# One-core decode attention with a gated MLP: the first sixteen output rows in four column groups, wide value products in seven batches, five filler matmuls fewer

## The chip, the core and the metric

The kernel runs on one core of one Trainium2 chip. The metric is the device time of one execution in microseconds (us). One execution was also taken with the hardware profiler; the line numbers below (L612 and so on) are those of the kernel before. Names used: PE is the matmul engine, with its weight loads shown apart (PEld), DVE the vector engine, ACT the scalar engine, POOL the general engine, and SP the engine that issues most DMAs.

## The reference

For eight sequences with one new token each, the layer norm of the input goes through a grouped-query attention with a window of W = 2048 cached positions (32 query heads over 8 key/value heads of 128), and beside it through a gated MLP; the two results are multiplied and added to the input. All tensors are bfloat16.

```python
W = min(4096, max(256, Sk // 4))          # Sk 8192 -> 2048
q = (xn @ wq)                             # 8 x 4096
scores = einsum("bhqd,bhkd->bhqk", q, k[:, :, Sk-W:]) * Dh ** -0.5
p = softmax(scores)
s = einsum("bhqk,bhkd->bhqd", p, v[:, :, Sk-W:]).reshape(B, Sq, Hq * Dh) @ wo
h = sigmoid(xn @ w_gate) * (xn @ w_up)
g = silu(h @ w_down)
out = x + s * g                           # x and xn: A_x and its layer norm
```

## The kernel before

**Transfers.** All large transfers are issued by SP on one queue, in the order of a list that is written out by hand (`todo`, taken off by `pump`): the MLP weights, `wq`, then for each of the 8 batches and 2 halves of the heads one K and one V tile of 2 MB, and last `wo` in four pieces of 16, 10, 4 and 2 rows. A row of `wo` here is 128 x 512 values, one on each partition, 128 KB. The tiles go into a ring of nine 2 MB slots, and a transfer is issued as soon as a slot that it needs has been given back; K runs three tiles ahead of V. The `wo` pieces need two adjacent slots and are issued when the last K tile has been transposed.

**Attention.** Every batch `b` has NU = 8 units `u` of K (two halves of the heads, four quarters of the window each). Per unit, PE transposes K (L484, two groups of 8, each copied out by DVE at L489) and multiplies with the queries (`scores`, L502). After a batch's last unit `row_max` takes the maxima on DVE and four exponentials on ACT (L522); `stat_rows`, `factor` and `spread` work out one scale for each head (small operations on DVE with fp32 transposes on PE at L534, L535, L578, all in the PSUM tile `m_ps`); `p_transposes` turns the probabilities (L591, copied by DVE at L596).

**Value products.** `value(b, i, c)` at L612 is the product of probabilities and V, in 16 chunks `c` for each half `i`. There are two forms. For `b < WIDE` (5) one matmul per half and chunk has 64 probability columns against 512 columns of V (64 column groups, two of which fill the array), and it also computes products that are not wanted; `combine` (L632, ACT) copies 128 x 512 out and `normalise` (L642) picks the wanted parts with four fp32 matmuls. For the other batches two matmuls have 32 probability columns against 256 columns of V each (four column groups fill the array); `combine` copies 128 x 256 and `normalise` makes two fp32 matmuls. `turn` (L660, L667) then puts the batch's result into its column of `oP_sb`. All batches share one accumulator `o_ps`, so the next batch's value products wait for the `combine` of the last.

The value products of batch `b` are spread over the units of batch `b + 2`, except for the end, which is written out from L700 on: the last unit of batch 5, `combine(5)`, all of batch 6 (`last - 1`) between `normalise(5)` and `turn(5)`, then batch 7 (`last`): its probabilities are turned in two halves, the first V half is multiplied in two groups of 8 chunks, and the second V half (the last V tile to land) last.

**Fillers.** `keep(n)` (L720) issues n matmuls of 128 x 480 into a tile that nobody reads. There are fourteen: 2 and 3 around the two groups of batch 7's first half, 2, 1 and 3 while batch 7's result is scaled, and 3 between the two halves of the output rows.

**Output.** `into` multiplies a 32-column left side by four 128-column quarters of a right side, two column groups at a time, with the even and odd quarters landing on shifted rows (the left side is read one column earlier for the second pair). The loop at the end makes 32 x 4 such matmuls from `oP_sb` and the rows of `wo` into `fin_ps` (64 x 128), and two DVE operations and two output DMAs follow. The same helper, with `pick_f` as the left side in fp32, gathers the four column groups of the MLP's product `d_ps` (L403, nineteen matmuls of 32 x 512 in four column groups, copied by ACT to `d_sb` at L432) into `b_ps`.

The reader needs in addition:

```python
value(last, 1, c) for c in range(CU)      # waits for the last V tile
keep(2); combine(last); normalise(last, l_ps[:, 0:Hq])
keep(1); turn(last, l_ps[:, P : P + RT]); keep(3)
```

Of the kernel before, what the change touches and what calls it, by code (L numbers as in the profile page):

```python
# [10 lines left out]
def kernel(  # L11
# [13 lines left out]
    nc = tc.nc  # L25
    P = 128
    B, _, D = A_x.shape
# [8 lines left out]
    G = 4  # L36
# [12 lines left out]
    f32 = mybir.dt.float32  # L49
# [8 lines left out]
    ktpool = ctx.enter_context(tc.tile_pool(name="ktpool", bufs=3))  # L58
# [4 lines left out]
    ps_t = ctx.enter_context(  # L63
        tc.tile_pool(name="ps_t", bufs=4, space=bass.MemoryType.PSUM)
    )
# [16 lines left out]
    weights = {}  # L82
# [53 lines left out]
    MT = 9  # L136
# [45 lines left out]
    RT = 32  # L182
    Z = 32
# [30 lines left out]
    for p, n, step in SEGS:  # L214
        nc.gpsimd.tensor_copy(
            out=sel[:, p : p + (n - 1) * step + 1 : step],
            in_=ident[:NSEL, at : at + n],
# [14 lines left out]
        out=which[:],  # L232
# [7 lines left out]
        out=side["t"].rearrange("p t n -> p (t n)"),  # L240
        out_offset=None,
        in_=B_w_down[:m0, :].rearrange("(p t) n -> p (t n)", t=SF),
# [7 lines left out]
        out=perm[:].rearrange("k (l p) -> k l p", l=G),  # L250
        in_=ident[:].rearrange("k (p l) -> k l p", l=G),
# [11 lines left out]
        out=rstd[:], in_=mv[:, 1:2], func=AF.Sqrt, bias=eps_t[:], scale=1.0  # L263
# [4 lines left out]
        out=xn_bf[:],  # L268
# [8 lines left out]
    for kt in range(KT):  # L277
        nc.tensor.transpose(  # L278
            out=xnT_ps[:, kt, :],
            in_=xn_bf[:].rearrange("b (p kt) -> b kt p", kt=KT)[:, kt, :],  # L280
# [6 lines left out]
    hT_sb = work.tile([P, MT + SF, Z], bf16, name="hT_sb")  # L287
    nc.gpsimd.memzero(hT_sb[:])
    oP_sb = work.tile([P, RT, 2 + Z], bf16, name="oP_sb")
# [12 lines left out]
    pick = consts.tile([P, RT], bf16, name="pick")  # L302
    pick_f = consts.tile([P, 2 + Z], f32, name="pick_f")
# [4 lines left out]
    with nc.allow_low_precision(reason="zeros and a one"):  # L308
        nc.vector.reduce_sum(
            out=band[:], in_=ident[:].rearrange("k (q t) -> k q t", t=RT), axis=AX.X  # L310
        )
        nc.vector.reduce_sum(
            out=pick[:], in_=ident[:].rearrange("k (q t) -> k t q", t=RT), axis=AX.X
        )
    nc.gpsimd.tensor_copy(out=pick_f[:, 2 : 2 + 2 * B : 2], in_=pick[:, :B])


    FC = 448
# [1 line left out]
    for k in range(F // FC):  # L320
        g_ps = ps_t.tile([B, FC], f32, name="g_ps", tag="t")
        for kt in range(KT):
            nc.tensor.matmul(  # L323
                g_ps[:],
                lhsT=xnT_sb[:, kt, :B],
                rhs=weights[("wg_sb", kt)][:, k * FC : (k + 1) * FC],
                start=(kt == 0),
                stop=(kt == KT - 1),
# [7 lines left out]
    for k in range(F // FC):  # L336
        u_ps = ps_t.tile([B, FC], f32, name="u_ps", tag="t")
        for kt in range(KT):
            nc.tensor.matmul(  # L339
                u_ps[:],  # L340
                lhsT=xnT_sb[:, kt, :B],
                rhs=weights[("wu_sb", kt)][:, k * FC : (k + 1) * FC],
                start=(kt == 0),
                stop=(kt == KT - 1),
            )
        nc.vector.tensor_tensor(  # L346
            out=h_bf[:B, k * FC : (k + 1) * FC],
# [5 lines left out]
    hT_ps = ps_m.tile([P, MT + SF, B], bf16, name="hT_ps", tag="m")  # L353
# [3 lines left out]
    for t, x in enumerate(cuts):  # L357
        nc.tensor.transpose(
            out=hT_ps[: rows[t], t, :], in_=x, identity=ident[:B, :B]
        )  # L360
    nc.vector.tensor_copy(out=hT_sb[:, :MT, :B], in_=hT_ps[:, :MT])
    hc_sb = work.tile([NSEL, SF, B], bf16, name="hc_sb")
    nc.scalar.copy(out=hc_sb[:], in_=hT_ps[:NSEL, MT:])

# [3 lines left out]
    def into(out_ps, lhsT, rhs, start=True, stop=True):  # L368
        for e in range(2):
            for g in range(NG):  # L370
                j = 2 * e + g
                nc.tensor.matmul(  # L372
                    out_ps[Z * g : Z * (g + 1), :],
                    lhsT=lhsT[:, 2 - e : 2 - e + Z],
                    rhs=rhs[:, j * P : (j + 1) * P],
                    start=(start and e == 0),
                    stop=(stop and e == 1),
                    tile_position=(0, Z * g),
                    skip_group_check=True,
                )  # L380

    q_ps = [ps_t.tile([P, D], f32, name="q_ps", tag="t") for _ in range(2)]
    for kt in range(KT):
        for e in range(2):
            for g in range(G):
# [3 lines left out]
                    lhsT=xnT_sb[:, kt, :],  # L389
                    rhs=weights[("wq_sb", kt)][:, c0 : c0 + D],  # L390
                    start=(kt == 0),
                    stop=(kt == KT - 1),
                    tile_position=(0, Z * g),
                    skip_group_check=True,
                )
    free(rows_of[("wq_sb", 0)])
    spot_ps = ps_t.tile([P, SF, B], f32, name="spot_ps", tag="t")
    nc.tensor.matmul(spot_ps[:], lhsT=sel[:], rhs=hc_sb[:], start=True, stop=True)
    nc.scalar.copy(out=hT_sb[:, MT:, :B], in_=spot_ps[:])
    d_ps = ps_s.tile([P, D], f32, name="d_ps", tag="s")  # L400
    for t in range(MT + SF):
        g = t % G
        nc.tensor.matmul(  # L403
            d_ps[Z * g : Z * (g + 1), :],
            lhsT=hT_sb[:, t, :],
            rhs=weights[("wd_sb", t)],
            start=(t < G),
            stop=(t >= MT + SF - G),
            tile_position=(0, Z * g),
            skip_group_check=True,  # L410
        )
    for e in range(2):
# [3 lines left out]
        for r in range(rep):  # L416
            nc.tensor.transpose(  # L417
                out=qT_ps[:, r].rearrange("p g z -> p (g z)"),
                in_=q_bf[:, r * Dh : (r + 1) * Dh],
# [3 lines left out]
            out=qm_sb[:, :, G * e : G * (e + 1), M0 : M0 + rep].rearrange(  # L423
                "p b g r -> p r g b"
            ),
            in_=qT_ps[:, :, :, :B],
# [21 lines left out]
        out=turn_rows[:].rearrange("k (x l r) -> k x l r", x=NU, l=G),  # L448
        in_=ident[:].rearrange("k (l x r) -> k x l r", x=NU, l=G),
    )  # L450
    sel_e = consts.tile([P, 2, Hq], f32, name="sel_e")
    for e in range(2):
        nc.vector.reduce_sum(
            out=sel_e[:, e, :].rearrange("k (i h) -> k i h", i=NQ),
            in_=ident_f[:].rearrange(
                "k (i m e h) -> k e i h m", i=NQ, m=NJ // 2, e=2
            )[:, e],
# [12 lines left out]
    kT = {}  # L470
# [80 lines left out]
    def factor(b):  # L551
        w = row.pop(b)
        own = small.tile([1, LI, NJ, rep], f32, name="own")
        nc.vector.tensor_tensor(
            out=own[:],
            in0=w[:],
            in1=sum_ps.rearrange("o (a j r) -> o a j r", a=LI, j=NJ),
            op=ALU.mult,
        )
        den = small.tile([1, LI, rep], f32, name="den")  # L560
        nc.vector.reduce_sum(
            out=den[:], in_=own[:].rearrange("o a j r -> o a r j"), axis=AX.X
        )
        nc.vector.reciprocal(out=den[:], in_=den[:])
        f = small.tile([1, NQ, NJ, G, rep], f32, name="f_row")
        nc.vector.tensor_tensor(
            out=f[:].rearrange("o i j l r -> o l i j r"),
            in0=w[:].rearrange("o (l i) j r -> o l i j r", i=NQ),
            in1=den[:]
            .rearrange("o (l i) r -> o l i r", i=NQ)  # L570
            .unsqueeze(3)
            .to_broadcast([1, G, NQ, NJ, rep]),
            op=ALU.mult,
        )
        row[b] = f
# [10 lines left out]
    def p_transposes(b, h):  # L586
        if h == 0:
            pT[b] = ppool.tile([P, CU, P], bf16, name="pT_sb")
        pT_ps = ps_t.tile([P, CH, P], bf16, name="pT_ps", tag="t")
        for c in range(CH):  # L590
            nc.tensor.transpose(  # L591
                out=pT_ps[:, c, :],
                in_=p_buf[b % 2][:, :, :, h * CH + c].rearrange("k p l -> k (p l)"),
                identity=turn_rows[:],
            )
        nc.vector.tensor_copy(out=pT[b][:, h * CH : (h + 1) * CH, :], in_=pT_ps[:])  # L596

    NM = NJ // 2
    NX = P // NQ
    WIDE = 5  # L600

    def value(b, i, c):
        v = v_tiles[(b, i)][0]
        if b < WIDE:
            rows = [slice(NX * i, NX * (i + 1))]
# [5 lines left out]
        for r, x in zip(rows, parts):  # L611
            nc.tensor.matmul(  # L612
                o_ps[r] if b < WIDE else o_ps[r, 0:2],
                lhsT=pT[b][:, c, r],
# [13 lines left out]
    def combine(b):  # L628
        del pT[b]
        n = NJ if b < WIDE else 2  # L630
        o = small.tile([P, NJ, Dh], f32, name="o_sb")
# [5 lines left out]
    def normalise(b, oT_ps=oT_ps):  # L637
        o = row.pop(b)
        sel = sel_j if b < WIDE else sel_e
        n = NJ if b < WIDE else 2  # L640
        for e in range(n):
# [76 lines left out]
    def keep(n):  # L718
        for _ in range(n):
            nc.tensor.matmul(  # L720
                idle_ps[:, : Hkv * (M0 + Z)],
                lhsT=ident[:],
                rhs=idle_in,
                start=True,
                stop=True,
            )

    keep(2)
    for c in range(CU // 2):
        value(last, 0, c)  # L730
    p_transposes(last, 1)
    keep(3)
    factor(last)
    normalise(last - 1)
    for c in range(CU // 2, CU):
# [10 lines left out]
    turn(last, l_ps[:, P : P + RT])  # L746
    keep(3)

    fin_ps = ps_s.tile([ZO, P], f32, name="fin_ps", tag="s")
    for t in range(RT):  # L750
        if t == 16:
            keep(3)
        into(fin_ps, oP_sb[:, t, :], weights[("wo_sb", t)], t == 0, t == RT - 1)

    prod = work.tile([ZO, P], f32, name="prod")
    nc.vector.tensor_tensor(out=prod[:], in0=gg_sb[:], in1=fin_ps[:], op=ALU.mult)
# [2 lines left out]
    for g, q in enumerate((q0, q1)):  # L759
        q.dma_start(  # L760
            out=out.flatten_outer_dims().rearrange(
                "b (e g n) -> g (b e) n", e=2, g=NG
            )[g],
            in_=y_bf[Z * g : Z * g + 2 * B, :],
# [31 lines left out]
```

## Time and profile before

| what | value |
|---|---|
| median of three runs | 198.56 us (198.26 to 198.57) |
| the profiled execution's own time | 198.86 us |
| its span (first to last instruction) | 197.1 us |
| around the span | 1.76 us |
| DMA traffic | 81.32 MB, mean 413 GB/s |
| PE, DVE, ACT, POOL busy | 163.4, 125.7, 40.8, 9.1 us |
| wide value product (128x64 weights, 512 columns) | 160 of them, mean 397 ns each |
| narrow value product (128x32 weights, 256 columns) | 192 of them, mean 273 ns each |

The durations of single matmuls overlap, since they are pipelined and run in different column groups; what one costs is read from the start of a block to the start of the next. The profile gives the granted PE clock as a share of full speed, and for each stretch the mean busy share of the 16 DMA engines and the rate. "Idle before" with a name is the time that the engine stood still and what ended it.

### The profile page before, as it was taken

The page shows a single profiled execution, that of the slowest core. Times are in us where ns is not written, and L with a number is a line of the kernel's source. Part 1 is how long each engine was busy: PE and PEld are TensorE (multiplying, and loading weights), DVE is VectorE, ACT ScalarE, POOL GpSimd, SP SyncE. Part 2 cuts the span into 40 slices and gives each one's busy share as a digit, 9 for nine tenths or more (in the row PEclk, how much of TensorE's full clock was granted, in tenths as well). Part 3 has the DMA queues.
Part 4 walks back from the last instruction along what each step waited for, and adds up shares of the span by engine and source line. Part 5 has one row for each costly group of instructions (what it writes and reads, how often), then busy time and mean ns, then how long its engine had stood idle before and what let it go on. Part 6 is the DMA issues. An engine that isn't in the chain of part 4 may idle for free.

```text
span 197.1 us, 4818 instructions
## 1 busy us (share of the span) xinstructions
PE 163.4 (83%) x2114; PEld 106.8 (54%) x2114; DVE 125.7 (64%) x247; ACT 40.8 (21%) x95; POOL 9.1 (5%) x31
## 2 busy tenths in 40 slices
PE   0029859999699999799979987999799998878883
PEld 0013423876576575456646654665467566655652
DVE  4540401999799796679667966796549878935201
ACT  0053003001701501600160016001600070071000
POOL 7910000000000000000000000000000000000000
PEclk9999966999999999999999999999879999999999
DMA  6999999999999999999999999999999999999990
GB/s 203 438 440 463 416 406 426 436 436 432 424 429 429 422 426 422 439 432 432 426 432 434 426 426 421 429 436 426 419 442 439 426 431 422 426 429 429 420 401 16
DMA packets 6148, 81.32 MB, mean 413 GB/s; under 512 B 808, under 2 KB 816, under 8 KB 1328
## 3 DMA queue, kind: packets, MB, share of 16 engines
q1 hardware_dynamic: 5936, 80.35, 96.0%
q0 software_dynamic: 144, 0.66, 0.8%
q8 instruction: 16, 0.26, 0.5%
q14 instruction: 4, 0.03, 0.0%
q10 hardware_dynamic: 48, 0.01, 0.0%
HBM read 81.67 MB, written 0.01 MB: 414 GB/s over the span
## 4 chain that ended last, share of the span: by engine, by line
DMA 65%; PE 25%; DVE 5%; ACT 3%; issue 1%; SPq 0%; ACTq 0%
DMA ring<-in_A_k_cache_dram 29%; DMA ring<-in_A_v_cache_dram 13%; PE kT_ps L484 13%; DMA ring<-in_A_wq_dram 11%; DMA ring<-in_A_wo_dram 10%; PE s_ps L502 4%; PE o_ps L612 3%; DMA ring<-in_B_w_gate_dram 3%; DVE kT_sb L489 2%; PE q_ps L387 2%; ACT p_buf L522 2%; PE fin_ps L372 1%; PE d_ps L403 1%; DVE pT_sb L596 1%; ACT L522 1%
## 5 line engine op out<-in xcount | busy, mean ns | idle before, releaser
L489 DVE COPY kT_sb<-kT_ps 128x1024 bf16<-128x1024 bf16 x128 | 84.3, 684 | 26.0 <-PE kT_ps L484 21.2
L484 PE MATMUL kT_ps<-perm,ring 128*128 128x128 bf16 x1024 | 73.4, 221 | 2.0 <-DMA ring<-in_A_k_cache_dram 2.0
L484 PEld LDWEIGHTS <-ring 128*128 128x128 bf16 x1024 | 59.5, 99 | 24.6 <-issue 18.3
L612 PE MATMUL o_ps<-ring,pT_sb 128*32 128x256 bf16 (+1 forms) x352 | 36.6, 330 | 6.6 <-DMA ring<-in_A_v_cache_dram 5.6
L502 PE MATMUL s_ps<-kT_sb,qm_sb 128*32 128x512 bf16 x256 | 25.8, 393 | 1.3 <-DVE kT_sb L489 1.1
L522 ACT ACTIVATE p_buf<-s_ps,st 32x512 bf16<-32x512 f32 x32 | 21.7, 679 | 15.5 <-DVE st L515 15.1
L612 PEld LDWEIGHTS <-pT_sb 128*32 128x32 bf16 (+1 forms) x352 | 12.4, 102 | 19.4 <-issue 17.6
L632 ACT ACTIVATE o_sb<-o_ps,fac 128x512 f32<-128x512 f32 (+1 forms) x8 | 4.9, 608 | 60.5 <-PE o_ps L612 60.5
L596 DVE COPY pT_sb<-pT_ps 128x1024 bf16<-128x1024 bf16 x16 | 10.8, 676 | 1.8 <-PE pT_ps L591 1.8
L502 PEld LDWEIGHTS <-qm_sb 128*32 128x32 bf16 x256 | 7.0, 93 | 8.1 <-issue 1.5
L591 PE MATMUL pT_ps<-turn_rows,p_buf 128*128 128x128 bf16 x128 | 10.7, 227 | 0.0
L591 PEld LDWEIGHTS <-p_buf 128*128 128x128 bf16 x128 | 9.4, 148 | 0.2 <-issue 0.2
L278 PE MATMUL xnT_ps<-ident,xn_bf 8*128 8x8 bf16 x4 | 0.3, 174 | 9.9 <-DVE xn_bf L267 9.9
L549 ACT ACTIVATE w_row<-w 1x128 f32<-1x128 f32 x8 | 2.5, 308 | 28.6 <-DVE w L542 28.6
L346 DVE TENSOR_TENSOR h_bf<-sig,u_ps 8x448 bf16<-8x448 f32 x4 | 2.4, 608 | 6.6 <-PE u_ps L339 6.1
L422 DVE COPY qm_sb<-qT_ps 128x128 bf16<-128x128 bf16 x2 | 1.4, 876 | 8.1 <-PE qT_ps L417 8.1
L323 PE MATMUL g_ps<-ring,xnT_sb 128*8 128x448 bf16 x16 | 5.7, 541 | 0.3 <-DVE xnT_sb L285 0.3
L522 ACT ACTIVATION_READ_ACCUMULATOR p_buf<-s_ps,st 32x1 f32 x32 | 5.9, 184 | 0.0
L515 DVE TENSOR_REDUCE st<-s_ps 128x1 f32<-128x512 f32 x8 | 5.5, 682 | 0.5 <-PE s_ps L502 0.5
L278 PEld LDWEIGHTS <-xn_bf 8*128 8x128 bf16 x4 | 0.2, 114 | 10.0 <-DVE xn_bf L267 10.0
L387 PE MATMUL q_ps<-ring,xnT_sb 128*32 128x512 bf16 x32 | 3.6, 629 | 2.4 <-DMA ring<-in_A_wq_dram 2.4
L642 PE MATMUL m_ps<-ident_f,o_sb 128*128 128x32 f32 x40 | 5.2, 272 | 0.0
(97 smaller groups left out, 97.0 us busy)
## 6 DMA issues: line engine op xcount, KB each, us to landing
ring<-in_A_k_cache_dram SPq DMA_DIRECT2D x16, 2048.0 KB, 28.5
ring<-in_A_v_cache_dram SPq DMA_DIRECT2D x16, 2048.0 KB, 30.4
ring<-in_A_wq_dram SPq DMA_DIRECT2D x1, 4096.0 KB, 21.6
ring<-in_A_wo_dram SPq DMA_DIRECT2D x1, 2048.0 KB
ring<-in_B_w_gate_dram SPq DMA_DIRECT2D x2, 896.0 KB, 6.0
ring<-in_B_w_up_dram SPq DMA_DIRECT2D x1, 1792.0 KB, 13.1
ring<-in_A_wo_dram SPq DMA_DIRECT2D x1, 1280.0 KB
ring<-in_B_w_down_dram SPq DMA_DIRECT2D x1, 1152.0 KB
```

Source lines behind the costliest of these rows:

```text
L323: nc.tensor.matmul(g_ps[:], lhsT=xnT_sb[:, kt, :B], rhs=weights[("wg_sb", kt)][:, k * FC : (k + 1) * FC], start=(kt == 0), stop=(kt == KT ...
L387: nc.tensor.matmul(q_ps[e][Z * g : Z * (g + 1), :], lhsT=xnT_sb[:, kt, :], rhs=weights[("wq_sb", kt)][:, c0 : c0 + D], start=(kt == 0), st ...
L484: nc.tensor.transpose(out=kT_ps[:, c, :], in_=k_sb[:, j * CU + h * CH + c, :], identity=perm[:],)
L489: nc.vector.tensor_copy(out=kT[(b, u)][:, h * CH : (h + 1) * CH, :], in_=kT_ps[:])
L502: nc.tensor.matmul(s_ps[b][NR * l : NR * (l + 1), :], lhsT=qm_sb[:, b, i * G + l, o : o + Z], rhs=t[:, :, PG * l : PG * (l + 1)], start=(u ...
L515: nc.vector.tensor_reduce(out=st[b][:], in_=s_ps[b][:], axis=AX.X, op=ALU.max, negate=True)
L522: nc.scalar.activation(out=p_buf[b % 2][rows, :, l, :], in_=s[rows, :].rearrange("k (c p) -> k p c", p=PG), func=AF.Exp, bias=st[b][rows, ...
L591: nc.tensor.transpose(out=pT_ps[:, c, :], in_=p_buf[b % 2][:, :, :, h * CH + c].rearrange("k p l -> k (p l)"), identity=turn_rows[:],)
L596: nc.vector.tensor_copy(out=pT[b][:, h * CH : (h + 1) * CH, :], in_=pT_ps[:])
L612: nc.tensor.matmul(o_ps[r] if b < WIDE else o_ps[r, 0:2], lhsT=pT[b][:, c, r], rhs=x, start=(c == 0), stop=(c == CU - 1), tile_position=(0 ...
L632: nc.scalar.activation(out=o[:, :n], in_=o_ps[:, :n], func=AF.Copy, scale=fac.pop(b)[:])
L642: nc.tensor.matmul(oT_ps, lhsT=o[:, e, :], rhs=sel[:, e], start=(e == 0), stop=(e == n - 1),)
```

## The change

Four things change.

1. `WIDE` goes from 5 to 7: batches 5 and 6 take the wide form of the value products, of `combine` and of `normalise`. Only batch 7 keeps the narrow form.
2. The first 16 of the 32 output rows go into a new PSUM tile `r_ps`: one matmul of 32 x 512 for each row, in four column groups. ACT copies `r_ps` to `r_sb` in fp32, and `into` with `pick_f` adds the four groups into `fin_ps` before the other 16 rows.
3. Fillers: `keep(2)` before batch 7's first group goes, `keep(3)` behind `p_transposes(last, 1)` becomes `keep(1)`, and `keep(3)` between the halves of the output rows becomes `keep(2)` behind the `r_ps` matmuls.
4. Since the results of the batches stand in every second column of `oP_sb`, `pick_f` now picks every second row of each group; so `hT_sb`, the left side of `d_ps`, is written to every second column as well.

The instruction orders of DVE, POOL and SP are otherwise as before; ACT has one instruction more (the copy of `r_ps`).

```diff
-    nc.gpsimd.tensor_copy(out=pick_f[:, 2 : 2 + 2 * B : 2], in_=pick[:, :B])
+    nc.gpsimd.tensor_copy(
+        out=pick_f[:, 2 : 2 + 2 * B : 2], in_=pick[:, : 2 * B : 2]
+    )
...
-    nc.vector.tensor_copy(out=hT_sb[:, :MT, :B], in_=hT_ps[:, :MT])
+    nc.vector.tensor_copy(out=hT_sb[:, :MT, : 2 * B : 2], in_=hT_ps[:, :MT])
...
-    nc.scalar.copy(out=hT_sb[:, MT:, :B], in_=spot_ps[:])
+    nc.scalar.copy(out=hT_sb[:, MT:, : 2 * B : 2], in_=spot_ps[:])
...
-    WIDE = 5
+    WIDE = 7
...
-    keep(2)
     for c in range(CU // 2):
         value(last, 0, c)
     p_transposes(last, 1)
-    keep(3)
+    keep(1)
     factor(last)
     normalise(last - 1)
...
+    RG = 16
+    r_ps = ps_t.tile([P, D], f32, name="r_ps", tag="t")
+    for t in range(RG):
+        g = t % G
+        nc.tensor.matmul(
+            r_ps[Z * g : Z * (g + 1), :],
+            lhsT=oP_sb[:, t, 2 : 2 + Z],
+            rhs=weights[("wo_sb", t)],
+            start=(t < G),
+            stop=(t >= RG - G),
+            tile_position=(0, Z * g),
+            skip_group_check=True,
+        )
+    keep(2)
+    r_sb = ktpool.tile([P, D], f32, name="r_sb", tag="kT")
+    nc.scalar.copy(out=r_sb[:], in_=r_ps[:])
     fin_ps = ps_s.tile([ZO, P], f32, name="fin_ps", tag="s")
-    for t in range(RT):
-        if t == 16:
-            keep(3)
-        into(fin_ps, oP_sb[:, t, :], weights[("wo_sb", t)], t == 0, t == RT - 1)
+    into(fin_ps, pick_f[:], r_sb[:], True, False)
+    for t in range(RG, RT):
+        into(fin_ps, oP_sb[:, t, :], weights[("wo_sb", t)], False, t == RT - 1)
```

## The prediction

> **What bounds the kernel now.** I read the page's slices first, then the chain of waits, then the stretches of the end, then the timeline of its last 25 us. The DMA engines are full from the second slice to the last but one, and the chain that ended last is mostly DMA; its last steps are these:
>
> ```profile
> 171.83 19.82 DMA ring<-in_A_wo_dram
> 191.65 0.04 issue
> 191.69 2.24 PE fin_ps L372 x64
> 193.93 0.02 issue
> 193.96 0.29 DVE prod L756
> ```
>
> So the output weights set the end. Where their data ends is seen in the stretches (columns: length, busy time of PE, PEld, DVE, ACT, POOL, then granted clock, DMA share, GB/s):
>
> ```profile
> 60.00:80.00 20.00, 19.59 (x252) 12.51 (x253) 16.80 (x32) 4.09 (x10) 0.00 (x0) 1.00 1.01 431
> ...
> 160.00:170.00 10.00, 9.33 (x153) 7.18 (x156) 8.25 (x18) 2.66 (x8) 0.00 (x0) 1.00 1.00 426
> ...
> 192.00:193.00 1.00, 1.00 (x40) 0.94 (x36) 0.00 (x0) 0.00 (x0) 0.00 (x0) 1.00 0.28 109
> ```
>
> At 109 GB/s in the last of them the bytes stop after about 0.26 us, at 192.26. The first sixteen rows of `wo` are seen by PE at 188.74, the next ten at 191.69. The second batch of 64 takes 2.24 us where the first took 1.96, so the last two pieces also land only just in time. PE is bound by landings at three places, and between them it has slack:
>
> ```profile
> 182.92 0.22 PE L578 MATMUL m_ps<-ident_f,f_row 1*128 1x1 f32 x1
> ...
> 183.79 1.92 PE L612 MATMUL o_ps<-ring,pT_sb 128*32 128x256 bf16 x32 [0.23 <-DMA ring<-in_A_v_cache_dram]
> ...
> 187.39 0.77 PE L720 MATMUL idle_ps<-qm_sb,ident 128*128 128x480 bf16 x3
> ...
> 188.74 1.96 PE L372 MATMUL fin_ps<-ring,oP_sb 128*32 128x128 bf16 x64 [0.59 <-DMA ring<-in_A_wo_dram]
> 190.64 0.32 PEld L720 LDWEIGHTS <-ident 128*128 128x128 bf16 x3
> ...
> 191.69 2.23 PE L372 MATMUL fin_ps<-ring,oP_sb 128*32 128x128 bf16 x64 [0.27 <-DMA ring<-in_A_wo_dram]
> ```
>
> The question is therefore not what PE saves, but whether it still arrives at 191.69 with the first sixteen rows behind it.
>
> **The part at the start** (`pick_f`, `hT_sb`): the same instructions with other strides, hidden twice: `hT_sb` is wanted before 31.3 us, while the stream runs on unhurried to 192. Were the cover gone, it would cost some tenths of the 0.23 us that the ACT copy at 31.48 takes. I take 0.
>
> **The stream.** The transfers, their order and SP's waits stay. `wo` is issued when K is transposed, at 171.44, and its first data can't start before about 183.8, where the last V tile is seen; a delay of under 1 us there costs nothing. No load follows.
>
> **Wide products, batch 5.** A block of 8 narrow matmuls takes 0.33 us to the start of the next operation (170.01 to 170.34), a block of 4 wide ones, the same work, 0.55 (156.67 to 157.22): 0.22 more. Blocks u = 0 to 2 lie before 164.04, where PE waits 0.56 us for K. Of u = 3 to 6, 0.9 us in all, half a microsecond goes into PE's 0.58 us wait for DVE at 172.74 and the rest into the 0.25 us before L578 at 169.09; DVE runs there without a gap and sets the pace. I take 0 up to 172.74; without that cover it is up to 0.4. From there on it counts. Block u = 7: +0.22. `combine(5)`: 0.688 instead of 0.475 us: +0.21. Behind it on ACT stand the four exponentials of batch 7, ended at 177.5 instead of 177.1, and on PE all of batch 6, which waits for `o_ps`: it starts 0.43 late, at 174.42.
>
> **Wide products, batch 6.** The marginal cost of a narrow matmul: 16 take 0.56 (174.88 to 175.44), 40 take 1.20 (175.56 to 176.76), so 27 ns each; 64 cost 1.73 us. Of the wide form only blocks of four exist. Lower bound: the fixed part of a block (0.33 less 8 x 0.027) is 0.11, which leaves 0.11 each; upper bound: 0.55/4 = 0.1375. In a long row the fixed part falls away as with the narrow form, so I take 0.11: 32 x 0.11 = 3.52, +1.79. (The Trainium skill, "TensorE: Matmul & The Clock Gate", section Back-to-back issue gap, gives about 131 ns for each 512-column matmul in a stream with weight loads; by that the end would come 0.67 us later than I forecast. The rows of this trace, 0.1375 with the switch in it, do not exclude it.)
>
> `normalise(5)` lies within: 8 fp32 passes take 0.87 (101.73 to 102.59) where 4 took 0.56: +0.31. Against this, PE's stand before L535 at 177.15 (0.39 from L534, 0.11 in mid-kernel) vanishes, since ACT is only 0.43 late: -0.28. PE starts batch 7's probabilities at 0.43 + 1.79 + 0.31 - 0.28 = 2.25 us late, 179.5.
>
> **Fillers before the last V tile.** Two go, two of three go; 0 saved. The first pair lay in PE's wait for DVE's copy L596 (value products at 178.70), the triple in its wait for `own` (L554, behind the same DVE queue) at 181.37. They could at most have saved their issue time, 4 x 0.2 us, if the waits were not there.
>
> **Up to the output.** `normalise(6)`: +0.31, so 2.56. Before, PE was ready for the last V tile at 183.51 (0.12 behind the start of L660 at 183.39) and began at 183.79: -0.28. The last 32 value products start 2.28 late, at 186.07. What follows up to the three fillers is a chain of PE, ACT and DVE with no other wait; the fillers' last issue slot ended at 187.99 (three of 0.2 from 187.39), now at 190.27. The first `wo` piece has been there since 188.74.
>
> **The new output.** `r_ps`: 16 matmuls, four at a time as in `scores` (0.33 a block, 0.11 of it fixed): the last four start 0.66 after the first and take 0.40: ends at 191.33. Upper bound the nineteen of `d_ps`, 1.84 us at a clock of 0.50: 0.5 us more. The ACT copy as `d_sb`: 0.05 lag and 0.586, to 191.97; `keep(2)` lies under it. The fp32 hand-over as `b_ps`: 0.14 lag (33.80 to 33.94) and 0.56 (33.94 to 34.50): 192.67. Then 64 matmuls without holes as in the first batch, 1.96: 194.63, against 193.93. Sum: +0.70 on a profiled execution of 198.86 (span 197.1 and 1.76 around it, which nothing touches), so 199.56; the median of the runs shown is 0.30 below that execution, so **199.2**.
>
> **The rivals.** (a) *Hidden*: between the start of `r_ps` and the first of the other rows lie 2.40 us, so PE may be up to 1.58 us late at the last V tile before anything shows. If waits that I counted as staying give way (the exponentials, L596, `own`), the lateness stays below that: 198.56. For it: PE idles nearly 3 us from 172 to 184; against it: each wait that ends there hangs on what PE itself did before. (b) *A faster stream*: the rate is 431 GB/s in stretches with wide products only, 426 from 160, when the narrow ones and their weight loads double; if these cost the stream that, 34 us x 5/431 = 0.4 us come back and all landings move up: 198.16. It decides only where PE is less than 1.2 us late as well; and the steps between stretches (432 at 150 to 160, 428 at 120 to 137) are as large. (c) *Dear wide products*: 0.1375 each, +0.88: 200.1. (d) *The clock*: PE's clock fell to 0.50 from 141.75 to 145.16, after a gap of 1.24 us (138.42 to 139.66) in a stretch of few full matmuls. In the new end, around 182.3 to 185.8, only one filler, eight fp32 passes and sixteen value products would run, gaps up to 0.9 us. If the clock falls at about 186, the 32 last value products take 1.9 us more: 201.1. The trace before had as thin a stretch, from 180.5 on, at 1.00.
>
> By the Trainium skill, same page, Part 1 on the clock gate, only idle gaps of some 3.4 us halve the clock, which would leave out (d). The trace disagrees: 1.24 us of idleness were enough here.
>
> **How the numbers follow.** Forecast 0.48, (a) 0.20, (b) 0.14, (c) 0.12, (d) 0.06. A measurement of this kernel tells about 0.2% (0.4 us) from no change. Slower by more: 0.42 of the forecast, (c) and (d): 0.60. Within: 0.06 of the forecast, 0.17 of (a), 0.04 of (b): 0.27. Faster: the rest, 0.13. The forecast's own range is 198.9 to 199.7 (lateness 0.4 to either side); with (a), (c) and the bounds of `r_ps` it is 198.3 to 200.3, which leaves out (d) and the lower half of (b).
>
> **What would show it.** Right: value products of batch 6 in about 3.5 us from 174.4; the last 32 starting near 186 with no wait for V; `r_ps` near 190.3 with no wait for `wo`; the ACT copy of `r_ps` near 0.59 and ended near 192; the rows from the seventeenth on starting near 192.7, after their weights landed (191.7), in 1.96 us. Wrong: a wait for `wo` ahead of row sixteen in the new trace (rival a); that wait ending before 191.4 (b); blocks of wide products at 0.1375 each (c); a clock below 1.00 after 180 (d).

## The result and the profile after

The changed kernel takes 200.48 us (median of six; 200.12 to 200.72 but for one execution at 203.41) against 198.52 us: 1.0098 times the time before, 95% interval 1.0087 to 1.0109. The prediction had the sign (slower) but 199.2 us, 0.64 more than before, where 1.96 were measured, and its range ended at 200.3. The ratio and its interval leave out the execution at 203.41, which counts as slow.

First the summary of the chain of waits of the changed kernel (shares of the span by engine, then by engine, tile and line):

```profile
DMA 58%; PE 33%; DVE 5%; ACT 2%; issue 1%; ACTq 0%
DMA ring<-in_A_v_cache_dram 44%; PE kT_ps L486 12%; DMA ring<-in_A_wq_dram 11%; PE o_ps L614 9%; PE s_ps L504 3%; DMA ring<-in_B_w_gate_dram 2%; PE m_ps L644 2%; DVE kT_sb L491 2%; PE q_ps L389 2%; PE pT_ps L593 1%; DVE pT_sb L598 1%; PE fin_ps L374 1%; ACT o_sb L634 1%; PE r_ps L754 1%; ACT q_bf L416 0%
```

`wo`, 10% of the chain before, is gone from it. The last transfer that anybody waits for is a V tile. After that the kernel is bound by PE and by the short DVE and ACT steps between its operations. The timeline of the end shows it (start, length, engine, line, operation, tile, form, count, and in brackets the idle time before and what ended it):

```profile
158.90 0.59 PE L614 MATMUL o_ps<-ring,pT_sb 128*64 128x512 bf16 x3 [1.23 <-DMA ring<-in_A_v_cache_dram]
...
164.08 0.62 PE L486 MATMUL kT_ps<-perm,ring 128*128 128x128 bf16 x8
...
173.21 0.40 PE L504 MATMUL s_ps<-kT_sb,qm_sb 128*32 128x512 bf16 x4
173.54 0.62 PE L614 MATMUL o_ps<-ring,pT_sb 128*64 128x512 bf16 x4
175.00 0.62 PE L614 MATMUL o_ps<-ring,pT_sb 128*64 128x512 bf16 x4 [0.84 <-ACT o_sb L634]
...
176.56 1.05 PE L614 MATMUL o_ps<-ring,pT_sb 128*64 128x512 bf16 x8
...
177.67 2.35 PE L614 MATMUL o_ps<-ring,pT_sb 128*64 128x512 bf16 x20
...
186.84 1.92 PE L614 MATMUL o_ps<-ring,pT_sb 128*32 128x256 bf16 x32
...
191.13 1.05 PE L754 MATMUL r_ps<-ring,oP_sb 128*32 128x512 bf16 x16
...
192.23 0.58 ACT L765 COPY r_sb<-r_ps 128x512 f32<-128x512 f32 x1 [2.91 <-PE r_ps L754]
...
192.87 0.63 PE L374 MATMUL fin_ps<-r_sb,pick_f 128*32 128x128 f32 x8 [0.18 <-ACT r_sb L765]
...
193.33 1.96 PE L374 MATMUL fin_ps<-ring,oP_sb 128*32 128x128 bf16 x64
```

Neither the 32 last value products nor the rows of `wo` show a wait for a transfer any more, and the last 64 matmuls run without holes, in 1.96 us. The lateness of PE against the trace before, step by step:

| start of | before | after | late | predicted late |
|---|---|---|---|---|
| last scores (L502) | 172.74 | 173.21 | 0.47 | 0 |
| first product of batch 6 | 173.99 | 175.00 | 1.01 | 0.43 |
| batch 7's probabilities turned (L591) | 177.26 | 180.16 | 2.90 | 2.25 |
| last 32 value products | 183.79 | 186.84 | 3.05 | 2.28 |
| first output rows | 188.74 | 191.13 | 2.39 | 1.53 |
| seventeenth output row | 191.69 | 193.33 | 1.64 | 0.98 |
| `prod` (L756) | 193.96 | 195.33 | 1.37 | 0.70 |

### The profile page after: what moved, and what is told of

Same layout as the page of the kernel before. It is cut to its first block, busy times and chain, and to the rows that moved or that the text cites. A ratio compares the mean times of both kernels' runs of the same rounds, so it can differ in the third digit from the quotient of the medians.

```text
span 198.5 us, 4617 instructions
## 1 busy us (share of the span) xinstructions
PE 164.7 (83%) x2013; PEld 105.9 (53%) x2013; DVE 125.9 (63%) x247; ACT 41.6 (21%) x96; POOL 9.1 (5%) x31
## 4 chain that ended last, share of the span: by engine, by line
DMA 58%; PE 33%; DVE 5%; ACT 2%; issue 1%; ACTq 0%
DMA ring<-in_A_v_cache_dram 44%; PE kT_ps L486 12%; DMA ring<-in_A_wq_dram 11%; PE o_ps L614 9%; PE s_ps L504 3%; DMA ring<-in_B_w_gate_dram 2%; PE m_ps L644 2%; DVE kT_sb L491 2%; PE q_ps L389 2%; PE pT_ps L593 1%; DVE pT_sb L598 1%; PE fin_ps L374 1%; ACT o_sb L634 1%; PE r_ps L754 1%; ACT q_bf L416 0%
## 5 line engine op out<-in xcount | busy, mean ns | idle before, releaser
L614 PE MATMUL o_ps<-ring,pT_sb 128*64 128x512 bf16 (+1 forms) x288 | 40.2, 367 | 6.8 <-DMA ring<-in_A_v_cache_dram 5.2
L614 PEld LDWEIGHTS <-pT_sb 128*64 128x64 bf16 (+1 forms) x288 | 11.8, 106 | 21.6 <-issue 19.2
L644 PE MATMUL m_ps<-ident_f,o_sb 128*128 128x32 f32 x56 | 7.5, 278 | 0.8 <-DVE own L556 0.8
L644 PEld LDWEIGHTS m_ps<-ident_f,o_sb 128*128 128x128 f32 x56 | 6.9, 195 | 1.5 <-DVE own L556 1.1
```

Of the source, the lines that this page charges most:

```text
L614: nc.tensor.matmul(o_ps[r] if b < WIDE else o_ps[r, 0:2], lhsT=pT[b][:, c, r], rhs=x, start=(c == 0), stop=(c == CU - 1), tile_position=(0 ...
L644: nc.tensor.matmul(oT_ps, lhsT=o[:, e, :], rhs=sel[:, e], start=(e == 0), stop=(e == n - 1),)
```

## The experiments

Three theories stood at the start. L: PE is late by the wide products of batches 5 and 6. H: the serial hand-over from PE over ACT to PE costs the time. F: the missing fillers cost it.

**WIDE back to 5 in the changed kernel.**

```diff
-    WIDE = 7
+    WIDE = 5
```

> The changed kernel with WIDE back at 5; the r_ps hand-over and the fewer fillers stay. Theory L (PE comes late to the output because of the wide products of batches 5 and 6; in the trace 3.05 us late at the last V tile): PE is again early, r_ps starts when the first wo piece lands (about 188.7), its 2.2 us to the first of the other rows end before 191.7, and the time is that of before, 198.5 us (within 0.3). Theory H (the serial hand-over PE, ACT, PE costs the time, 2.2 us on the path): stays at 200 or above. Theory F (the five fillers, by the clock or the pace of PE): stays at 200 or above too.

The run gave 198.41 us, ratio to before 0.9993 (0.9972 to 1.0015). The waits for `wo` are back, in PE's timeline of this run:

```profile
188.20 1.05 PE L754 MATMUL r_ps<-ring,oP_sb 128*32 128x512 bf16 x16 [0.55 <-DMA ring<-in_A_wo_dram]
...
191.17 2.30 PE L374 MATMUL fin_ps<-ring,oP_sb 128*32 128x128 bf16 x64 [0.61 <-DMA ring<-in_A_wo_dram]
```

So the hand-over and the missing fillers cost nothing when PE is in time; H and F fall as causes of the loss, and L stands. The second line also shows the second `wo` piece at 191.17, half a microsecond earlier than in the trace before (191.69).

**WIDE 6 in the changed kernel** (batch 5 wide, batch 6 narrow).

```diff
-    WIDE = 7
+    WIDE = 6
```

> The changed kernel with WIDE 6: only batch 5 wide. Theory L: the lateness is that of batch 5 alone, 0.47 up to the last scores, 0.32 at combine(5), 0.2 for its copy, 0.3 for normalise(5), less the 0.3 that PE waited for the sums and the 0.3 that it waited for V: about 0.8 us at the last V tile, below the 1.6 that are hidden: 198.5 us (within 0.4). A cost per wide batch (L in proportion, no hidden part) would give 199.5. H and F: 200 or above.

The run gave 198.37 us, ratio 1.0016 (0.9991 to 1.0041): the lateness is hidden in most executions, though three of twelve were at 199.5 to 201.5. The last 32 value products start at 184.63. That is 0.84 late against the trace before, where PE waited for V at that place; the expectation had 0.8. Against the 183.28 of WIDE 5, which has no such wait, it is 1.35. Those three executions were not traced.

**WIDE 7 alone in the kernel before.**

```diff
-    WIDE = 5
+    WIDE = 7
```

> The kernel before with WIDE 7 alone: all fillers, the first sixteen rows as before. Theory L: the first of the output rows starts at 191.1 instead of 188.7, then 1.96 and three fillers (2.65 us to the start of the second half) and 1.96: the profiled end 1.8 later, so 200.3 to 200.9 us, as slow as the changed kernel or 0.4 slower. H: 198.5, since the hand-over is absent. F: 198.5, since all fillers are there.

The run gave 202.16 us, ratio 1.0163 (1.0134 to 1.0191). L is right in the sign, since wide products alone make it slow with all fillers in place, but its range ended at 200.9: four of six executions lie at 202.1 to 202.4 and two at 200.6 and 200.8. The trace, that of the execution at 202.37, shows a fall of the clock (stretches: length, busy time of PE, PEld, DVE, ACT, POOL, granted clock, DMA share, GB/s):

```profile
158.00:158.50 0.50, 0.00 (x0) 0.00 (x0) 0.50 (x1) 0.44 (x1) 0.00 (x0) 1.00 1.08 459
...
161.00:161.50 0.50, 0.50 (x9) 0.50 (x6) 0.29 (x1) 0.18 (x2) 0.00 (x0) 0.50 1.15 492
...
164.00:164.50 0.50, 0.50 (x9) 0.50 (x8) 0.17 (x1) 0.00 (x0) 0.00 (x0) 0.62 1.14 459
```

PE waited 1.25 us for batch 5's V, and two microseconds later its clock stood at half for one window of 3.4 us. Where PE still has waits behind such a fall, they take it up. The trace of the changed kernel has one at 102 to 106 (0.63, 0.50, 0.50 and 0.67 in windows of 1 us) and the run with fewer turns below has none there, and both meet batch 5's V at 158.90. Behind 161 the wide kernel has no such wait left, and the last scores start at 174.79, 1.58 after those of the changed kernel.

**The fillers put back into the changed kernel.**

```diff
+    keep(2)
     for c in range(CU // 2):
         value(last, 0, c)
     p_transposes(last, 1)
-    keep(1)
+    keep(3)
...
-    keep(2)
+    keep(3)
     r_sb = ktpool.tile([P, D], f32, name="r_sb", tag="kT")
```

> The changed kernel with the fillers put back (2 before batch 7's first group, 3 behind its second turn, 3 behind r_ps). Theory L: all of them lie in waits that stand in the trace of the changed kernel (0.79 for L598, 0.76 for own, 0.65 for the ACT copy): no change, 200.5 us (within 0.3). F: 1 to 2 us less, 198.5 to 199.5. H: no change.

The run gave 200.55 us, ratio 1.0112 (1.0099 to 1.0126): no gain. F falls from the other side too.

**Batch 6 wide, batch 5 narrow.**

```diff
-    WIDE = 7
+    WIDES = (0, 1, 2, 3, 4, 6)
...
-        if b < WIDE:
+        if b in WIDES:
```

> The changed kernel with batch 6 wide and batch 5 narrow. Theory L (lateness adds up over the two batches and shows only beyond what is hidden): PE is late by batch 6 alone, 1.8 for its 32 wide products and 0.3 for normalise(6), less the 0.3 that it waited for the sums: 1.8 us late behind normalise(6), 1.5 at the last V tile, about the edge of what is hidden: 198.4 to 198.9 us. A theory that batch 6 alone costs what the changed kernel lost (since only its products stand in the written-out end): 200.0 to 200.5.

Median 199.11, ratio 1.0041 (1.001 to 1.0071), but in groups: six executions at 198.47 to 198.72, two at 199.5 and 199.6, four at 200.2 to 200.4. The traced one (198.58) has the last 32 products at 185.18, 1.90 late against WIDE 5, and PE meets the seventeenth row at 191.67 without a wait for `wo`, which with WIDE 5 was there at 191.17: the margin is used up, and the span is 196.8 against 196.6. The two batches add up: 1.35 and 1.90 are 3.25, and the changed kernel's start at 186.84 is 3.56 behind 183.28. The 0.3 between is PE's wait for the sums (L537; 176.57 to 176.95 with WIDE 5 and 0.11 in the others), which each single batch swallows and the two together only once. What makes the groups at 199.5 and above is open: none of them was traced, and their mean clocks (0.966 to 0.974) do not stand apart from those of the first group (0.963 to 0.983).

**Fillers in the wait for batch 5's V**, added to WIDE 7 alone and to the changed kernel.

```diff
+    def fill(n):
+        fill_ps = ps_t.tile([P, 512], f32, name="fill_ps", tag="t")
+        for _ in range(n):
+            nc.tensor.matmul(fill_ps[:, : Hkv * (M0 + Z)], lhsT=ident[:],
+                rhs=qm_sb[:, 0].rearrange("k h m -> k (h m)"), start=True, stop=True)
...
+            if b == B - 1 and u == 0:
+                tasks[3].append(lambda: fill(6))
```

> The kernel before with WIDE 7, and six fillers where PE waits 1.25 us for batch 5's V (ahead of the first value products in the last batch's loop). Theory D (in the run of WIDE 7 alone, the granted clock fell to half for one window right after that wait, and since PE has no slack from there on, 1.6 us of it reach the end): the runs around 202.2 us go, all lie at 200.4 to 201.0. Against D (the scatter of WIDE 7 alone has another cause, or the fillers' 1.2 us come on top): a median of 202 or above.

> The changed kernel with the same six fillers in the wait for batch 5's V. Theory D: median 200.1 to 200.6 as the changed kernel, and no run above 201 (one of its six was at 203.4). Against D: runs above 201 as before, or 1 us more in all of them.

WIDE 7 alone with the fillers: 200.69 us, four executions at 200.60 to 200.79, ratio 1.0103 (1.0053 to 1.0152). The group at 202.2 is gone, as theory D has it. The changed kernel with them: 200.27, ratio 1.0097 (1.0072 to 1.0121); eight of ten at 200.17 to 200.61, two at 201.07 and 201.28. D expected none above 201, so one wait filled is not all of it. Between the two kernels 0.42 us are left. In the traces PE needs 2.60 us from the first output row to the seventeenth in the old form (191.15 to 193.75) and 2.20 in the new one (191.16 to 193.36). But 0.71 of the 2.60 are the three fillers between the halves (193.04 to 193.75); the rows themselves take 1.89. So the new hand-over gains nothing by itself when PE is late: it gains by having its fillers under the ACT copy.

**All nine remaining fillers out, WIDE 5.**

```diff
-    WIDE = 7
+    WIDE = 5
...
-    keep(1)
...
-    keep(2)
...
-    keep(1)
...
-    keep(3)
...
-    keep(2)
```

> The changed kernel with WIDE 5 and all nine fillers that are left taken out. Theory that the fillers carry nothing here: 198.4 us as with them. Theory that they hold the clock: the clock falls to half somewhere from 178 on, the 32 last value products or the 64 of the last rows take 1.9 us more, and the time is 199.3 to 200.5 in some or all runs.

Median 198.84, ratio 1.0028 (1.0 to 1.0055), from 198.27 to 200.36. The mean clock was 0.983 to 0.991 in the three executions at 198.27 to 198.35, 0.952 and 0.946 in those at 199.8 and 200.36, though not every execution in between follows it. With the nine fillers all eleven executions lay at 198.30 to 198.60. So the fillers as a whole keep the time steady, probably by the clock, which is not shown (the traced execution was one of those at 198.3); the five that the change took can be spared, as the run with WIDE 5 and the other nine shows.

**Fewer turns between the column-group forms.** Batch 5's value products in five blocks instead of eight.

```diff
-            if b >= 2:
+            if b >= 2 and b < B - 1:
                 tasks[2 * u + 3].append(lambda u=u: values_some(b - 2, u))
+            if b == B - 1 and u % 2 == 0:
+                if u > 0:
+                    tasks[2 * u + 3].append(lambda u=u: values_some(b - 2, u - 1))
+                tasks[2 * u + 3].append(lambda u=u: values_some(b - 2, u))
```

> The changed kernel with batch 5's value products in five blocks instead of eight: chunks 0 and 1 with the first unit as before, then four chunks at every second unit, the last two in the written-out end. The work is the same; only the number of turns between scores (32-column groups) and wide products (64-column groups) falls by three. Theory S (each such turn costs 0.11 to 0.12 us, which is why a wide block costs 0.33 more than a narrow one and not 0.22): the last scores start 0.33 to 0.36 us earlier after the landing of batch 5's V (13.95 instead of 14.3), and the time falls to about 200.1 us (199.9 to 200.3). Against S: no difference, 200.5 us.

Four executions are at 199.73 to 200.03, two at 201.5 and 202.0, which were not traced; median 199.98, ratio 1.0113 (1.0077 to 1.0149). In the trace batch 5's V is met at 158.90 as in the changed kernel, and the last scores start 0.49 earlier. PE's timeline of this run:

```profile
161.29 0.40 PE L504 MATMUL s_ps<-kT_sb,qm_sb 128*32 128x512 bf16 x4
161.62 0.62 PE L486 MATMUL kT_ps<-perm,ring 128*128 128x128 bf16 x8
...
162.97 1.05 PE L614 MATMUL o_ps<-ring,pT_sb 128*64 128x512 bf16 x8
163.96 0.62 PE L486 MATMUL kT_ps<-perm,ring 128*128 128x128 bf16 x8
...
171.74 1.05 PE L614 MATMUL o_ps<-ring,pT_sb 128*64 128x512 bf16 x8
172.72 0.40 PE L504 MATMUL s_ps<-kT_sb,qm_sb 128*32 128x512 bf16 x4
```

Scores followed at once by transposes take 0.33, the same as scores followed by wide products (172.72 to 173.05); scores followed by narrow products, which have the 32-column form too, take 0.22. Eight wide matmuls in one block take 0.98, two blocks of four 1.10. So each turn to another column form costs 0.11 to 0.12. The three turns that fell are seen one after the other: the transposes behind the first double block start 0.12 earlier than in the changed kernel (163.96 against 164.08), those behind the second 0.25 (168.32 against 168.57), and 0.12 of what is left comes with the third. The last 0.13 is no turn: in the changed kernel the last scores wait for DVE's copy, which ends at 173.16. Theory S fits.

**No wide products, then one and two wide batches.** The first was to show whether less PE work gains anything.

```diff
-    WIDE = 7
+    WIDE = 0
```

> The changed kernel with no wide products at all. Theory L: all the PE work that falls away lies in waits for the stream: 198.3 to 198.5 us, no better than with five wide batches. A theory that any wide batch costs something (that before already paid): 198.0 or less.

The run without wide products gave 199.50 us, ratio 1.0063 (1.005 to 1.0076): slower, which neither theory had. PE was early, but the chain of this run ends so:

```profile
173.42 20.42 DMA ring<-in_A_wo_dram
193.85 0.04 issue
193.89 0.41 PE fin_ps L374 x8
```

The last two `wo` rows landed at 193.89; PE had waited 0.90 for them. One packet of the instruction queue, 16 KB, started on a DMA engine between 191.5 and 192.0, while the last rows were in transfer. Two more runs with fewer PE instructions were to put it later.

```diff
-    WIDE = 7
+    WIDE = 1
```

```diff
-    WIDE = 7
+    WIDE = 2
```

> The changed kernel with one wide batch. In the run without wide products the last two wo rows landed 0.9 us late (193.89), and a 16 KB instruction packet lay on one DMA engine between 191.5 and 193, just ahead of it. One wide batch has 64 PE instructions fewer (4 KB, a quarter of a packet; one packet comes about every 10 us), so the packet comes some 2.5 us later, about 194.4. Theory I (the packet held up the last landing): 198.3 to 198.6 us. Theory N (narrow products in the early batches cost time by themselves): 199.2 to 199.5.

> The changed kernel with two wide batches: the packet some 5 us later than with none, behind the end of the wo transfers. Theory I: 198.3 to 198.6 us. Theory N: 199.0 to 199.3.

One wide batch: 198.52, ratio 1.0004 (0.9994 to 1.0013). The packet came half a microsecond later (192.0 to 192.5), not 2.5, and the landing was in time. Two: 198.74, ratio 1.0018 (1.0004 to 1.0031), seven of ten executions at 198.44 to 198.90 and three at 199.3 to 199.5, above the expectation. The trace is one of those three. Its packet started between 194.0 and 194.5, and its list of DMA issues (last column: us from issue to landing) has

```profile
out_dram<-y_bf SPq DMA_DIRECT2D x1, 4.0 KB, 2.4
out_dram<-y_bf ACTq DMA_DIRECT2D x1, 4.0 KB, 2.5
```

where the changed kernel and the one before have 1.4 and 1.5. `y_bf` was computed at 193.75, no later than with one wide batch (193.84); only the output was a microsecond late. Theory N falls, since one wide batch is as fast as five. Theory I is not shown: in the traces of the kernel before and of WIDE 5 a packet started between 191.0 and 191.5, in those of one wide batch and of WIDE 6 between 192.0 and 192.5, all among the last transfers, and no row of `wo` was 0.9 late. So a packet there does not hold the rows up wherever it lies, and whether it did so without wide products is open; it could not be removed by itself. The two executions at 199.52 with two wide batches have spans of 197.0 and 196.6, so most of their excess lies outside the span, and no trace of them was kept.

No version beat the kernel before: one wide batch, WIDE 5 and WIDE 6 in the changed kernel are its equals.

## Why the prediction was right and wrong

**Right: what bounds, and the way it went.** The output weights set the end before, the saving in the first sixteen rows fell into waits, and the wide products made PE late enough to show. The marginal price of a wide matmul was right: twelve more of them cost 1.29 (0.99 for eight, 2.28 for twenty), 0.108 each against the 0.11 taken. The fillers were worth nothing, as said. The hand-over took 2.20 us from the first row to the seventeenth where 2.40 were counted. Rival (c), 0.1375 for each wide matmul, is refuted; (a) did not come about; and (b) is not borne out: the queue of the loads moved its last bytes between 192.5 and 193.0 in the changed kernel as with WIDE 5 (5.6% and 3.5% of the engines' time there). In the trace before it was still busy there too (12.8%), so the bytes did not stop at 192.26, as the prediction read.

**Wrong: the term "Wide products, batch 5".** "I take 0 up to 172.74" measured 0.47, for two reasons, the price of a block and the cover. The price taken was 0.22 more per block; the true one is 0.33: a narrow block behind scores, also in 32-column groups, needs no turn and adds 0.22 to the scores and transposes around it; a wide one adds 0.55. The prediction compared only the blocks' own lengths, from their start to the next operation (0.33 and 0.55), and missed the 0.11 that the narrow form saves ahead of it.

The cover was misjudged as well. (Its sum did not close either: of 0.9 us it put half a microsecond into one wait, and 0.4 do not fit into the other, of 0.25.) The prediction saw that DVE "sets the pace", and still counted PE's waits for DVE as room for PE's delay. The chain of waits of the changed kernel leaves PE behind the second transposes of u = 3, runs over DVE, and returns only at the last scores (start, length, engine, tile, line):

```profile
166.25 0.57 PE kT_ps L486 x8
166.82 0.02 issue
166.84 0.69 DVE kT_sb L491
...
171.87 1.30 DVE kT_sb L491 x2
173.16 0.04 issue
173.21 0.40 PE s_ps L504 x4
```

In the trace before, the same copy is the second of this pair:

```profile
165.82 1.34 DVE L489 COPY kT_sb<-kT_ps 128x1024 bf16<-128x1024 bf16 x2
```

Alone a copy takes 0.69 there, so the second started about 166.47, as soon as its transposes (165.81 to 166.43) were done. From there on DVE has no gap in either trace, but for about 0.1 us ahead of 171.87 in the changed kernel. So what PE loses ahead of 166.84 goes through DVE whole: 0.04 is left of the first blocks behind PE's vanished wait for K (164.04 to 164.08), and 0.33 is the wide block of u = 3. With the 0.1 ahead of 171.87 that makes the 0.47. The waits of 0.25 and 0.58 are waits for this same chain; they took up most of what PE lost in u = 4 to 6, but nothing that DVE had lost already. By the same rows even the 0.22 that the prediction took for u = 3 would have come through; that is an estimate, no run shows it.

**What else was mis-sized.** The same turn is in the block of u = 7 (0.11) and in the two `normalise` steps, whose eight passes take 1.01 to the next column-group product (175.55 to 176.56) and not the 0.87 read where transposes follow; with the small rest of those steps 0.2. Together that is 0.77 at the last value products. Up to the first output rows 0.09 comes on top, the hand-over takes 0.20 less, and 0.67 is left at the end. The Trainium skill, "TensorEngine Tiling (Array Packing)", section Tiling Modes, says that changing the tiling mode drains the engine; these runs agree in so far as each change has a price of 0.11 to 0.14; the drain itself no run here shows.

**Wrong: the margin and the step to the median.** "PE may be up to 1.58 us late" came from one execution whose landings were late. Its span was 197.1, while 79 of 82 executions of the same kernel in the later jobs had 196.5 to 196.9, and the second `wo` piece, met at 191.69 there, was met at 191.06 to 191.24 in the five other traces where PE waits for it. So about half a microsecond of the margin was that execution's own. The last step of the sum took 0.30 off for the median, as if that lateness were in the changed kernel as well; but there PE waits for no `wo`, so it must not come off. Trace against trace the change costs 1.37; the medians differ by 1.96 because the trace before was 0.34 above its median and the trace after 0.25 below.

**The clock, rival (d).** It stood at 0.06 and with the wrong place (186). The fall was seen at 161 to 164, in the trace of WIDE 7 alone, and it cost 1.6 us there. The prediction set a gap of 1.24 us against what the Trainium skill says in "TensorE: Matmul & The Clock Gate", Part 1, that idle gaps of some 3.4 us halve the clock. These traces do not bear out the gap alone either. The fall at 161 came behind a gap of 1.25, but none came behind 1.23 at the same place in the changed kernel, behind 1.49 with WIDE 5 or behind 1.81 with two wide batches (each ended between 158.7 and 159.0). What else decides it stays open.

## What to carry to other kernels

When a load-bound kernel gets more work on an engine that has slack, find the last landing that engine waits for and add up its work from there to the end. Here that was batch 5's V at 158.9, and not the end of the stream. A wait for another engine is room for more work only if that engine does not itself wait for the work that grows. Price a block by what it adds between its neighbours, since a form that differs from theirs pays for the turn on both sides. Read a hidden margin from several executions, not from the one that was traced.

## What the runs showed of the hardware

A 16 KB instruction packet takes 0.9 to 1.1 us on one DMA engine in most traces, once 1.4 (11.6% to 13.5%, once 17.3%, of 16 engines' time in half a microsecond), and comes about every ten microseconds in this kernel. With such a packet between 191.5 and 192.0 `wo` landed 0.9 us late (193.89), and with one between 194.0 and 194.5 the output needed 2.4 and 2.5 us instead of 1.4 and 1.5; that the packets were the cause is not shown.

A turn between matmuls of different column forms costs PE 0.11 to 0.14 us here. And a clock that fell to half for 3.4 us cost nothing where PE waited again afterwards (102 to 106 in the changed kernel), and 1.6 us where it didn't (161 to 164 in WIDE 7 alone).
